# Attention with a gated mixer behind it: value projections by float32r parts, one h, one sum on ScalarE, another order at both ends

## The chip, the cores and the metric

The kernel runs on one core of a Trainium2 chip. The engines are called as in the profile: PE (TensorE, the matmuls), PEld (its weight loads), DVE (VectorE), ACT (ScalarE), POOL (GpSimd) and SP (SyncE, which issues most DMAs). The metric is the device time of one execution in microseconds, as the median of several runs.

## The reference

Four batches are computed, each with 12,288 queries of 128 channels and a field of 384 x 32 keys that is pooled 4 x 4 to 768.

```
kv_pool = mean over 4 x 4 of kv;   k = v = kv_pool @ w_sr          # 768 x 128
s = (q @ k.T) / sqrt(128);  s -= s.max(-1)
a = exp(s);  a /= a.sum(-1) + 1e-09
x = a @ v                                                         # 12288 x 128
gate = sigmoid(sum over k < 5 of conv_w[k] * x[row + k - 4])      # per channel, along the rows
out = (gate * (x @ w_val)) @ w_out
```

## The kernel before

**Tiling.** Channels lie on the 128 partitions. A group is 512 queries of one batch (24 groups per batch, 96 in all, numbered `gi`), and it has four tiles `j` of 128 queries. The loop at L655 goes through the tiles one step at a time; `mj` is the step within a group, counted one step behind `j` (`LAG`). Nothing reorders the instructions: each engine takes its own in the order in which the loop's body writes them, and the stages of one group are spread over eight passes of the loop. In the pass `gi`:

- PE makes the scores of the next tile (L358): six float32r matmuls of 384 columns, three products (high by high, high by low, low by high) for each half of the 768 keys. DVE takes the row maximum (L383), ACT the exponential with its sum (L396), DVE adds 1e-9 and scales that sum to z (L403) and inverts it (L405), ACT writes the float16 high part of the weights (L420) and DVE the low part (L424). SP transposes both by DMA (L415).
- For the group `gi - 2` PE makes av with 18 float16 matmuls of 512 columns (L436), spread over the four steps; for `gi - 3` ACT writes x (L451) into a tile that holds two groups and four columns of the group ahead (the halo).
- For the pairs of groups around `gi - 4` POOL makes the convolution: five taps (L465) and four additions (L470) of 1024 columns, over eight steps.
- For `gi - 6`, at `mj == 2`, ACT makes the tanh of the gate and PE the value projection `g_val` (L512), a float32 matmul of 512 columns; DVE makes `h = (tanh + 1) * val` (L518) in two halves of 256, at `mj` 2 and 3. For `gi - 7` PE makes the out projection (L523), ACT writes it out of PSUM (L533), and every four groups SP stores them.
- For `gi + 2` ACT and POOL split the queries: ACT casts to the high part qh (L340), POOL subtracts to the low part ql (L345).

While one batch runs, the loop slips in the set-up of the next one's keys and values piece by piece; around the change of a batch POOL has values to convert as well (L259, L262).

**Start.** Before the loop 14 pieces of keys and values are pooled and projected. `portion` turns finished pieces into keys and values: ACT writes kh (L161), DVE kl (L164), ACT the scaled values vt (L169) and their sums (L186). PE runs idle transposes in between (`warming`).

**Tail.** Behind the loop the last seven groups, n7 to n1, are written out by hand: the value and out projections that are left, av of the last two groups, the convolution of n4, n2 and n1 on ACT and DVE (L487, L491), and that of n3 on POOL (L498, L502).

Of the kernel before, what the change touches and what calls it, by code (L numbers as in the profile page):

```python
# [27 lines left out]
def attn_moe_kernel(ctx, tc, qT, kvT, w_sr, w_moe, outT):  # L28
# [37 lines left out]
    wval, wout, cwt = wm[:, 0:C], wm[:, C:2 * C], wm[:, 2 * C:]  # L66

# [200 lines left out]
    LAG = 1  # L268
# [126 lines left out]
    def expo(g, j):  # L395
        nc.scalar.activation(out=g.s[j], in_=g.s[j], func=AF.Exp, bias=g.nm.pop(j),  # L396
                             accum_out=g.z[j])

    def norm(g, j):

        g.r[j] = small.tile([P, 1], F32, name="r")
        z = small.tile([P, 1], F32, name="z")
        nc.vector.tensor_scalar(out=z, in0=g.z.pop(j), scalar1=1e-9, scalar2=2.0 ** -15,  # L403
                                op0=ALU.add, op1=ALU.mult)
        nc.vector.reciprocal(out=g.r[j], in_=z)  # L405
# [104 lines left out]

    def g_val(g, m, c0=0, c1=GQ):
        nc.tensor.matmul(m, wval, g.x[:, HALO + c0:HALO + c1], start=True, stop=True)  # L512
        return m

    def g_h(th, m, name="h", h=None):
        if h is None:
            h = work.tile([C, GQ], F32, name=name, bufs=2 if name == "h" else 1)
# [29 lines left out]
    for b in range(B):  # L547
        for i in range(NG):
            g = Group()
            g.i, g.b, g.t0, g.st = len(groups), b, i * GQ, states[b]  # L550
            g.s, g.nm, g.z, g.r, g.hl, g.pt = {}, {}, {}, {}, None, None
            g.nm2 = {}
            groups.append(g)
# [30 lines left out]
    convert = load_moe()  # L584
# [25 lines left out]
    for n, i in enumerate(order):  # L610
        pool_kv(st, i)
        finish()
        if n in (0, 6, 8):
            base, m = n, bank_pair()[:, 0] if n else misc()
        if n in ends:
            project(st, m, base * PC, ends[n] * PC, (n + 1) * PC)
        if n == 9:
            warm = misc()
        if n in (9, 10, 12):
            warming(3)  # L620
        if n == WHOLES - 3:
# [25 lines left out]
    g_ql(at(0), 2 * P, GQ)  # L647
    finish()
# [5 lines left out]
    held, CATCH_UP = [], (B - 1) * NG + 9  # L654
    for t in range(NT * G + LAG):  # L655
# [92 lines left out]
    half = GQ // 2
    two = lambda: (lambda p: (p[:, 0], p[:, 1]))(bank_pair())
    one = lambda: bank_pair()[:, 0]  # L750
# [3 lines left out]
    spare = [t[:, c:c + GQ] for t in idle for c in range(0, 3 * GQ, GQ)]  # L754

    def gate_tile(name):
        return spare.pop() if name == "th2" else work.tile([C, GQ], F32, name=name)

    def av_bank():
        return ps_av.tile([C, GQ], F32, name="av")  # L760
# [3 lines left out]
    a0, a1 = two()  # L764
    n6.m, n5.m = g_val(n6, a0), g_val(n5, a1)
    av_slice(n2, 0, 18)
    n6.th, n5.th = g_tanh(n6.gate), g_tanh(n5.gate, gate_tile("th2"))
    halo(n4, n6, nc.scalar)
    acc4 = one()
    conv_first(n4, acc4)  # L770
    n7.m = g_out(n7.h, misc())
    gate3 = conv_pool(n3)
    n6.h = g_h(n6.th, n6.m)
    n5.h = g_h(n5.th, n5.m, h=spare.pop())
    conv_rest(n4, acc4)
    new_x(n2)
    g_x(n2, n2.av)
    halo(n2, n4, nc.scalar)
    acc2 = one()
    conv_first(n2, acc2)  # L780
# [15 lines left out]
    g_x(n1, avs[0], 0, half)  # L796
    n4.m = g_val(n4, one())
    acc1 = one()
    conv_first(n1, acc1[:, :half], 0, half)
    conv_rest(n1, acc1[:, :half], 0, half)  # L800
    n2.th = g_tanh(acc2, gate_tile("th2"))
    n3.m = g_val(n3, av_bank())
    n4.h = g_h(n4.th, n4.m)
    g_x(n1, avs[1], half, GQ)
    conv_first(n1, acc1[:, half:], half, GQ)
    conv_rest(n1, acc1[:, half:], half, GQ)
    n3.th = g_tanh(gate3, gate_tile("th"))
    n2.m = g_val(n2, misc())
    n1.m = g_val(n1, one())
    n4.m = g_out(n4.h, n4.m)  # L810
    n3.h = g_h(n3.th, n3.m, h=spare.pop())
    n1.th = gate_tile("th2")
    for c in (0, half):
        g_tanh(acc1[:, c:c + half], n1.th[:, c:c + half])
    n2.h = g_h(n2.th, n2.m)
    n3.m = g_out(n3.h, n3.m)
    h = work.tile([C, 2 * GQ], F32, name="tap1", bufs=1)
    hs = [g_h(*(t[:, c:c + half] for t in (n1.th, n1.m)), h=h[:, c:c + half]) for c in (0, half)]
    out_tile(n4)
    g_evac(n4, n4.m)  # L820
    n2.m = g_out(n2.h, n2.m)
# [5 lines left out]
    for h, c in zip(hs, (0, half)):  # L827
        g_evac(n1, g_out(h, one()[:, :half]), c, c + half)
        store(n1, c, c + half)
# [28 lines left out]
```

## Time and profile before

| | |
|---|---|
| median of 3 runs | 995.91 us (995.52 to 996.45) |
| the profiled execution | 996.03 us, of which the trace's span is 994.3 |
| PE busy | 964.1 us, 97% of the span |
| DVE busy | 942.3 us, 95% |
| ACT busy | 908.7 us, 91% |
| POOL busy | 867.6 us, 87% |

A busy share is a mean over the whole span: it says neither where an engine was idle nor whether that cost time. The chain that ended last goes back from the last instruction to what released each step, so its shares tell which engine's work the end hung on. A float32 matmul of 512 columns stands in the program's order once and in the trace as two instructions ("x2").

### The profile page before, as it was taken

How to read it: one execution, taken by the hardware profiler on the slowest of the kernel's cores; microseconds unless marked ns; L12 is line 12 of the kernel's file. 1: busy time of each engine (PE TensorE's matmuls, PEld its weight loads, DVE VectorE, ACT ScalarE, POOL GpSimd, SP SyncE). 2: the span in 40 equal slices, each digit the busy share in tenths (PEclk: the TensorE clock that was granted, in tenths of full speed). 3: DMA queues.
4: the chain of work that ended last, by engine and by line, in shares of the span. 5: the costliest groups of instructions: out<-in, count | busy, mean ns of one | idle time of the engine just before them, and what ended most of it. 6: DMA issues, size and time to landing. Idle time of an engine off the chain costs nothing.

```text
span 994.3 us, 14764 instructions
## 1 busy us (share of the span) xinstructions
PE 964.1 (97%) x4523; PEld 650.2 (65%) x4523; DVE 942.3 (95%) x1934; ACT 908.7 (91%) x1599; POOL 867.6 (87%) x654
## 2 busy tenths in 40 slices
PE   4789999999999999999999999999999999999998
PEld 3566666666666666666666666666666666666664
DVE  6999999999999999999999999999999999999996
ACT  2889999999999999999999999999999999999995
POOL 2759899888999989899899998989899989988993
PEclk9899999999999999999999999999999999999999
DMA  9999999999999999999999999999999999999996
GB/s 348 270 213 226 193 174 254 237 227 228 238 252 235 242 255 223 244 227 246 219 244 240 254 240 233 240 217 223 202 218 227 201 210 250 233 203 216 190 204 169
DMA packets 610367, 227.79 MB, mean 229 GB/s; under 512 B 594544, under 2 KB 595696, under 8 KB 604528
## 3 DMA queue, kind: packets, MB, share of 16 engines
q1 hardware_dynamic: 610288, 226.84, 108.4%
q8 instruction: 37, 0.61, 0.2%
q14 instruction: 42, 0.34, 0.1%
HBM read 50.66 MB, written 25.17 MB: 76 GB/s over the span
## 4 chain that ended last, share of the span: by engine, by line
PE 87%; DVE 6%; ACT 4%; DMA 1%; issue 1%; SPq 0%; ACTq 0%; DVEq 0%
PE s L358 36%; PE av L436 35%; PE m L523 8%; PE m L512 7%; DVE hl L424 3%; ACT hl L420 2%; DMA pt<-in_kv 1%; DVE nm L383 1%; DVE pool L119 1%; ACT s L396 1%; DVE r L405 0%; DVE s L491 0%; ACT qh L340 0%; PE m L224 0%; DVE h L518 0%
## 5 line engine op out<-in xcount | busy, mean ns | idle before, releaser
L470 POOL TENSOR_TENSOR acc<-acc,tap 128x1024 f32<-128x1024 f32 x184 | 436.7, 2373 | 7.2
L436 PE MATMUL av<-pt,vh 128*128 128x512 f16 (+1 forms) x1152 | 407.9, 380 | 4.2 <-ACT x L451 4.1
L424 DVE SCALAR_TENSOR_TENSOR hl<-s,r,hl 128x768 f16<-128x768 f32 x384 | 388.2, 1011 | 9.2 <-ACT hl L420 8.7
L420 ACT ACTIVATE hl<-s,r 128x768 f16<-128x768 f32 x384 | 345.8, 900 | 45.6 <-ACT qh L340 17.7
L383 DVE TENSOR_REDUCE nm<-s 128x1 f32<-128x768 f32 x382 | 362.1, 948 | 8.9
L396 ACT ACTIVATE s<-s,nm 128x768 f32<-128x768 f32 x384 | 335.5, 874 | 8.8 <-DVE nm L393 0.9
L358 PE MATMUL s<-kh,qh 128*128 128x384 f32 x764 | 267.6, 431 | 5.5 <-DVE z L403 2.7
L436 PEld LDWEIGHTS <-vh 128*128 128x128 f16 x1164 | 113.2, 97 | 163.0 <-issue 74.0
L436 PE MATMUL av<-pt,vl 128*128 128x512 f16 (+1 forms) x576 | 217.7, 378 | 0.0
L465 POOL TENSOR_SCALAR tap<-x,wm 128x1024 f32<-128x1024 f32 x184 | 204.2, 1124 | 0.0
L358 PE MATMUL s<-kh,ql 128*128 128x384 f32 x764 | 195.3, 337 | 0.0
L358 PE MATMUL s<-kl,qh 128*128 128x384 f32 x764 | 195.3, 337 | 0.0
L358 PEld LDWEIGHTS s<-kh,qh 128*128 128x128 f32 x764 | 144.7, 191 | 62.1 <-DVE hl L424 4.8
L345 POOL TENSOR_TENSOR ql<-q,qh 128x512 fp32r<-128x512 f32 (+1 forms) x97 | 123.0, 1268 | 34.8 <-ACT qh L340 34.8
L358 PEld LDWEIGHTS s<-kl,qh 128*128 128x128 f32 x764 | 139.1, 189 | 0.0
L358 PEld LDWEIGHTS s<-kh,ql 128*128 128x128 f32 x764 | 138.7, 189 | 0.0
L436 PEld LDWEIGHTS <-vl 128*128 128x128 f16 x582 | 57.2, 98 | 86.0 <-issue 64.6
L465 POOL TENSOR_SCALAR acc<-x,wm 128x1024 f32<-128x1024 f32 x46 | 51.5, 1119 | 48.6 <-ACT x L451 48.0
L523 PE MATMUL m<-h,wm 128*128 128x512 f32 x182 | 92.9, 591 | 0.2
L512 PE MATMUL m<-x,wm 128*128 128x512 f32 x182 | 92.8, 591 | 0.0
L405 DVE RECIPROCAL r<-z 128x1 f32<-128x1 f32 x384 | 63.0, 164 | 13.2
L518 DVE SCALAR_TENSOR_TENSOR h<-th,m 128x256 f32<-128x256 f32 x180 | 74.7, 415 | 0.5 <-ACT hl L420 0.3
(110 smaller groups left out, 661.9 us busy)
## 6 DMA issues: line engine op xcount, KB each, us to landing
q<-in_q SPq DMA_DIRECT2D x23, 1024.0 KB, 5.9
out<-o SPq DMA_DIRECT2D x22, 1024.0 KB, 4.7
kvt<-in_kv SPq DMA_DIRECT2D x21, 768.0 KB, 5.3
pt<-in_kv SPq DMA_DIRECT2D x12, 384.0 KB, 7.0
o<-in_kv SPq DMA_DIRECT2D x3, 768.0 KB, 9.5
pt<-hl SPq DMA_TRANSPOSE x98, 10.1
out<-o SPq DMA_DIRECT2D x3, 512.0 KB, 2.7
kvt<-in_kv SPq DMA_DIRECT2D x2, 384.0 KB, 7.3
```

The lines of the kernel that those rows point to most:

```text
L345: nc.gpsimd.tensor_tensor(out=g.ql[:, c0:c1], in0=g.q[:, c0:c1], in1=g.qh[:, c0:c1].bitcast(F32), op=ALU.subtract)
L358: nc.tensor.matmul(g.s[j][:, h], a[:, sl], k[:, h * HALF:(h + 1) * HALF], start=(i == 0), stop=(i == 2))
L383: nc.vector.tensor_reduce(out=nm, in_=g.s[j], axis=AX.XY, op=ALU.max, negate=True)
L396: nc.scalar.activation(out=g.s[j], in_=g.s[j], func=AF.Exp, bias=g.nm.pop(j), accum_out=g.z[j])
L420: nc.scalar.activation(out=part(g, j, 0), in_=g.s[j], func=AF.Copy, scale=g.r[j])
L424: nc.vector.scalar_tensor_tensor(out=part(g, j, 1), in0=g.s.pop(j), scalar=g.r.pop(j), in1=part(g, j, 0), op0=ALU.mult, op1=ALU.subtract)
L436: nc.tensor.matmul(out, g.st[v][:, k * P:(k + 1) * P], g.pt[:, j0:j1, a * NCH + k], start=(i == 0), stop=(i == len(AV_ORDER) - 1))
L465: nc.gpsimd.tensor_scalar(out=t, in0=g.two[:, k:k + 2 * GQ], scalar1=cwt[:, k:k + 1], scalar2=1.0, op0=ALU.mult, op1=ALU.mult)
L470: nc.gpsimd.tensor_tensor(out=g.acc, in0=g.acc, in1=t, op=ALU.add)
L512: nc.tensor.matmul(m, wval, g.x[:, HALO + c0:HALO + c1], start=True, stop=True)
L518: nc.vector.scalar_tensor_tensor(out=h, in0=th, scalar=1.0, in1=m, op0=ALU.add, op1=ALU.mult)
L523: nc.tensor.matmul(m, wout, h, start=True, stop=True)
```

## The change

- **Sum on ACT.** The z of tile 1 of each group is made by ACT, right behind the exponential; that of the other three tiles stays on DVE.
- **One h.** The two halves of h become one instruction of 512 columns at `mj == 3`, and its tile has one buffer in place of two.
- **Value projections by parts.** For a chosen group (`gi` being the pass, the group is `gi - 5`) x is split into a float32r high part xh and low part xl, and the projection is three float32r products with the parts of the weights (`wvh`, `wvl`, split once on POOL). It is so for one group in four (those with `gi % 4 == 3`, 17 of them, where POOL makes xh), for every second group from group 74 on (`SUMLESS`, where DVE makes xh), and in the tail for n6, n4 and n2 (n4 and n2 with xh from ACT). POOL makes xl each time, behind ql.
- **Start.** The idle transposes of the last two pieces are issued once in place of twice, the scaling of the values of the pieces 8 to 13 goes from ACT to DVE, and the sums of that portion stand behind the last keys.
- **Tail.** The order is another: n5's value projection ahead of n6's, the out projections of n6 and n5 behind av of n1, and the store of groups 84 to 87 behind the loop.

```diff
     def expo(g, j):
         nc.scalar.activation(out=g.s[j], in_=g.s[j], func=AF.Exp, bias=g.nm.pop(j),
                              accum_out=g.z[j])
+        if j == 1:
+            z = small.tile([P, 1], F32, name="z")
+            nc.scalar.activation(out=z, in_=g.z[j], func=AF.Copy, scale=2.0 ** -15,
+                                 bias=1e-9 * 2.0 ** -15)
+            g.z[j] = z
...
+    def split_x(g, names=None):
+        if names:
+            g.xh, g.xl = (work.tile([C, GQ], F32R, name=n) for n in names)
+        else:
+            g.xh, g.xl = (work.tile([C, GQ], F32R, name=n, bufs=1) for n in ("xh", "xl"))
+        x = g.x[:, HALO:HALO + GQ]
+        if names:
+            nc.scalar.copy(out=g.xh, in_=x)
+        elif g.i < SUMLESS:
+            nc.gpsimd.tensor_copy(out=g.xh, in_=x)
+        else:
+            nc.vector.tensor_copy(out=g.xh, in_=x)
+        return lambda: nc.gpsimd.tensor_tensor(out=g.xl, in0=x, in1=g.xh.bitcast(F32),
+                                               op=ALU.subtract)
+
     def g_val(g, m, c0=0, c1=GQ):
+        if g.xh is not None:
+            for i, (w, x) in enumerate(((wvh, g.xh), (wvl, g.xh), (wvh, g.xl))):
+                nc.tensor.matmul(m, w, x, start=(i == 0), stop=(i == 2))
+            return m
...
-        warming(4)
-    finish()
+    warming(4)
+    later.pop(0)()
+    rest = later[1:]
+    later.clear()
     row_max_half(at(0), 0, 0)
+    nc.vector.tensor_scalar_mul(out=st["vt"][:, 8 * PC:WHOLES * PC], in0=late, scalar1=1.0 / RR)
     portion(3, m, WHOLES, PIECES)
...
+    later[:0] = rest
     finish()
...
-        if vg and mj > 1:
-            sl = slice((mj - 2) * GQ // 2, (mj - 1) * GQ // 2)
-            g_h(vg.th[:, sl], vg.m[:, sl], h=vg.h[:, sl])
+        if vg and mj == 3:
+            vg.h = g_h(vg.th, vg.m)
...
+        if mj == 2 and gi > 7 and (gi % 4 == 3 or gi % 2 and gi - 5 >= SUMLESS):
+            low = split_x(at(gi - 5))
...
+        if mj == 3 and low:
+            low()
+            low = None
...
-    n6.m, n5.m = g_out(n6.h, a0), g_out(n5.h, a1)
-    conv_rest(n2, acc2)
-    n4.th = g_tanh(acc4, gate_tile("th"))
-    avs = av_bank()[:, :half], misc()[:, :half]
+    n4.th = g_tanh(b[:, 0], th_tile())
     new_x(n1)
-    for n, c in enumerate((0, half)):
-        j = c // P
-        av_range(n1, avs[n], 0, len(AV_ORDER), j, j + NT // 2)
+    for m, k in ((turned, 0), (last, half)):
+        av_range(n1, m[:, :half], 0, len(AV_ORDER), k // P, k // P + NT // 2)
+    g_x(n1, turned[:, :half], 0, half)
+    conv_first(n1, a[:, 0, :half], 0, half)
+    conv_rest(n1, a[:, 0, :half], 0, half)
+    n4.m = g_val(n4, b[:, 1])
+    n2.th = g_tanh(c[:, 0], spare.pop())
+    n6.m, n5.m = g_out(n6.h, b[:, 0]), g_out(n5.h, c[:, 0])
```

PE in the loop, around the value projection of a chosen group (s are scores, m the projection's bank, av follows). Before, and after:

```order
L358 MATMUL s<-kl,qh 128x384 x2
L358 MATMUL s<-kh,ql 128x384 x2
L512 MATMUL m<-x,wm 128x512
L436 LDWEIGHTS vh
L436 MATMUL av<-pt,vh 128x512
```

```order
L366 MATMUL s<-kl,qh 128x384 x2
L366 MATMUL s<-kh,ql 128x384 x2
L544 MATMUL m<-xh,wvh 128x512
L544 MATMUL m<-xh,wvl 128x512
L544 MATMUL m<-xl,wvh 128x512
L451 LDWEIGHTS vh
L451 MATMUL av<-pt,vh 128x512
```

The one matmul became three at the same place, and its operands come from xh and xl in place of x.

POOL around the end of a pass whose group is split, where a batch begins before, in the middle of a batch after (acc and tap belong to the convolution, vh and vl to the next batch's values):

```order
L470 TENSOR_TENSOR acc<-acc,tap_2836 128x1024
L259 CAST vh<-v 128x256
L262 TENSOR_TENSOR vl<-v,vh 128x256
L345 TENSOR_TENSOR ql<-q,qh 128x512
L460 COPY x<-x 128x4
```

```order
L485 TENSOR_TENSOR acc<-acc,tap_1906 128x1024
L485 TENSOR_TENSOR acc<-acc,tap_1908 128x1024
L535 CAST xh<-x 128x512
L353 TENSOR_TENSOR ql<-q,qh 128x512
L538 TENSOR_TENSOR xl<-x,xh 128x512
L475 COPY x<-x 128x4
```

The cast stands ahead of ql and the subtraction behind it, ahead of the next pair's halo and taps.

DVE in the last stage, in the steps `mj` 2 and 3 (hl is the low part, nm the row maximum). Before, and after:

```order
L424 SCALAR_TENSOR_TENSOR hl<-s,r,hl 128x768
L403 TENSOR_SCALAR z<-s 128x1
L405 RECIPROCAL r<-z 128x1
L383 TENSOR_REDUCE nm<-s 128x1
L518 SCALAR_TENSOR_TENSOR h<-th,m 128x256
L424 SCALAR_TENSOR_TENSOR hl<-s,r,hl 128x768
L403 TENSOR_SCALAR z<-s 128x1
L405 RECIPROCAL r<-z 128x1
L383 TENSOR_REDUCE nm<-s 128x1
L518 SCALAR_TENSOR_TENSOR h<-th,m 128x256
```

```order
L439 SCALAR_TENSOR_TENSOR hl<-s,r,hl 128x768
L418 TENSOR_SCALAR z<-s 128x1
L420 RECIPROCAL r<-z 128x1
L391 TENSOR_REDUCE nm<-s 128x1
L537 CAST xh<-x 128x512
L439 SCALAR_TENSOR_TENSOR hl<-s,r,hl 128x768
L418 TENSOR_SCALAR z<-s 128x1
L420 RECIPROCAL r<-z 128x1
L391 TENSOR_REDUCE nm<-s 128x1
L552 SCALAR_TENSOR_TENSOR h<-th,m 128x512
```

The cast stands where the first half of h stood, the whole h where the second half stood.

## Rows read from the trace of the kernel before

**Rows 1.** Page: busy time by engine; chain by engine; a group with its idle.

```profile
PE 964.1 (97%) x4523; PEld 650.2 (65%) x4523; DVE 942.3 (95%) x1934; ACT 908.7 (91%) x1599; POOL 867.6 (87%) x654
PE 87%; DVE 6%; ACT 4%; DMA 1%; issue 1%; SPq 0%; ACTq 0%; DVEq 0%
...
L420 ACT ACTIVATE hl<-s,r 128x768 f16<-128x768 f32 x384 | 345.8, 900 | 45.6 <-ACT qh L340 17.7
```

**Rows 2.** Busy us by engine in two stretches; last clock, DMA share, GB/s.

```profile
core 0: us, PE busy (x) PEld busy (x) DVE busy (x) ACT busy (x) POOL busy (x), PEclk, DMA share, GB/s
85.00:245.00 160.00, 160.00 (x754) 107.99 (x753) 156.15 (x331) 150.31 (x265) 144.91 (x105) 1.00 1.08 219
755.00:965.00 210.00, 210.00 (x986) 140.93 (x985) 199.20 (x387) 200.13 (x343) 190.46 (x133) 1.00 1.06 215
```

**Rows 3.** Timeline of two groups: start, duration, engine, line, operation.

```profile
802.00 1.02 PE L512 MATMUL m<-x,wm 128*128 128x512 f32 x2
...
809.14 4.80 POOL L470 TENSOR_TENSOR acc<-acc,tap 128x1024 f32<-128x1024 f32 x2
...
811.82 1.02 PE L512 MATMUL m<-x,wm 128*128 128x512 f32 x2
...
812.95 0.42 DVE L518 SCALAR_TENSOR_TENSOR h<-th,m 128x256 f32<-128x256 f32 x1
813.29 1.01 DVE L424 SCALAR_TENSOR_TENSOR hl<-s,r,hl 128x768 f16<-128x768 f32 x1
```

**Rows 4.** Chain of waits, last stage: start, duration, engine, line, instructions.

```profile
961.73 1.31 PE av L436 x6
...
963.04 1.04 PE s L358 x6
...
967.94 0.86 PE m L512 x2
```

**Rows 5.** Groups by shape, whole run: busy time, mean ns, idle before and releaser.

```profile
L345 POOL TENSOR_TENSOR ql<-q,qh 128x512 fp32r<-128x512 f32 x95 | 121.5, 1279 | 29.3 <-ACT qh L340 29.3
...
L518 DVE SCALAR_TENSOR_TENSOR h<-th,m 128x256 f32<-128x256 f32 x180 | 74.7, 415 | 0.5 <-ACT hl L420 0.3 <-ACT th L508 0.2
...
L403 DVE TENSOR_SCALAR z<-s 128x1 f32<-128x1 f32 x384 | 57.2, 149 | 2.4 <-ACT s L396 1.2
...
L498 POOL TENSOR_SCALAR tap<-x,wm 128x512 f32<-128x512 f32 x5 | 3.4, 692 | 2.1 <-ACT x L451 1.8
...
L518 DVE SCALAR_TENSOR_TENSOR h<-th,s 128x512 f32<-128x512 f32 x2 | 1.4, 684 | 1.2 <-ACT x L458 1.2
...
L458 ACT COPY x<-x 128x4 f32<-128x4 f32 x2 | 0.4, 182 | 0.0
...
L169 ACT ACTIVATE vt<-av 128x96 f32<-128x96 f32 x1 | 0.3, 252 | 0.0
```

**Rows 6.** Timeline at the start: a DVE pair beside a POOL subtraction.

```profile
25.95 0.49 DVE L88 TENSOR_SCALAR tap<-acc 128x261 int32<-128x261 int32 x2
...
26.14 1.42 POOL L345 TENSOR_TENSOR ql<-q,qh 128x512 fp32r<-128x512 f32 x1 [2.11 <-ACT qh L340]
```

**Rows 7.** Timeline of the first keys: ACT's piece of values, and PE's first score.

```profile
21.98 0.41 ACT L169 ACTIVATE vt<-s 128x288 f32<-128x288 f32 x1 [1.25 <-DVE kl L164]
...
22.98 0.19 PEld L378 LDWEIGHTS s<-kh,qh 128*128 128x128 f32 x1 [0.69 <-ACT kh L161]
```

**Rows 8.** Chain of waits in the tail: PE's last av, DVE's next conv row.

```profile
978.96 1.98 PE av L436 x18
...
981.98 0.50 DVE s L491
```

**Rows 9.** Timeline of the tail: DVE's conv rows.

```profile
977.95 3.13 DVE L491 SCALAR_TENSOR_TENSOR s<-x,wm,s 128x512 f32<-128x512 f32 x4 [1.04 <-ACT s L487]
```

**Rows 10.** Timeline where batch two begins: POOL's ql, PE's value projection.

```profile
273.07 1.28 POOL L345 TENSOR_TENSOR ql<-q,qh 128x512 fp32r<-128x512 f32 x1
...
277.27 1.02 PE L512 MATMUL m<-x,wm 128*128 128x512 f32 x2
```

More of the change, by code (lines that the diff above doesn't have):

```diff
@@ L66, in attn_moe_kernel, with split_weights @@
     wval, wout, cwt = wm[:, 0:C], wm[:, C:2 * C], wm[:, 2 * C:]
+    wvh, wvl = (const.tile([C, C], F32R, name=n) for n in ("wvh", "wvl"))
+    def split_weights():
+        return [
+            lambda: nc.gpsimd.tensor_copy(out=wvh, in_=wval),
+            lambda: nc.gpsimd.tensor_tensor(out=wvl, in0=wval, in1=wvh.bitcast(F32),
+                                            op=ALU.subtract),
+        ]
     def load_moe():
@@ L397, in expo @@
                              accum_out=g.z[j])
+        if j == 1:
[3 more added lines that the diff above has]
+            g.z[j] = z
     def norm(g, j):
         g.r[j] = small.tile([P, 1], F32, name="r")
-        z = small.tile([P, 1], F32, name="z")
-        nc.vector.tensor_scalar(out=z, in0=g.z.pop(j), scalar1=1e-9, scalar2=2.0 ** -15,
-                                op0=ALU.add, op1=ALU.mult)
+        z = g.z.pop(j)
+        if j != 1:
+            total, z = z, small.tile([P, 1], F32, name="z")
+            nc.vector.tensor_scalar(out=z, in0=total, scalar1=1e-9, scalar2=2.0 ** -15,
+                                    op0=ALU.add, op1=ALU.mult)
         nc.vector.reciprocal(out=g.r[j], in_=z)
@@ L516, in g_h @@
         if h is None:
-            h = work.tile([C, GQ], F32, name=name, bufs=2 if name == "h" else 1)
+            h = work.tile([C, GQ], F32, name=name, bufs=1)
         nc.vector.scalar_tensor_tensor(out=h, in0=th, scalar=1.0, in1=m,
@@ L626, in attn_moe_kernel @@
             portion(cuts[n][0], m, cuts[n][1], n + 1)
+            late = m[:, :(n + 1 - cuts[n][1]) * PC]
     score_half(at(0), 1, 0)
@@ L745, in attn_moe_kernel, with th_tile @@
             store_last(held.pop(0), 4)
+    while held:
+        store_last(held.pop(0), 4)
     n1, n2, n3, n4, n5, n6, n7 = groups[:-8:-1]
     half = GQ // 2
-    two = lambda: (lambda p: (p[:, 0], p[:, 1]))(bank_pair())
-    one = lambda: bank_pair()[:, 0]
+    a, b, c = (bank_pair() for _ in range(3))
+    turned = ps_av.tile([C, GQ], F32, name="av")
+    last = misc()
     idle = [kvp.tile([C, 2, R, PC * R], F32, name="kvt").rearrange("c n r x -> c (n r x)")
             for _ in range(2)]
[L754 to L760, printed above, removed]
+    spare = [t[:, k:k + GQ] for t in idle for k in range(0, 3 * GQ, GQ)]
+    spare += [work.tile([C, 2 * GQ], F32, name="acc", bufs=2)[:, :GQ]]
+    def th_tile():
+        return work.tile([C, GQ], F32, name="th")
     new_x(n3)
     g_x(n3, n3.av)
[L764 to L767, printed above, removed]
+    n5.m, n6.m = g_val(n5, a[:, 1]), g_val(n6, a[:, 0])
+    av_range(n2, turned, 0, len(AV_ORDER))
+    n6.th, n5.th = g_tanh(n6.gate, th_tile()), g_tanh(n5.gate, spare.pop())
     halo(n4, n6, nc.scalar)
-    acc4 = one()
-    conv_first(n4, acc4)
-    n7.m = g_out(n7.h, misc())
+    conv_first(n4, b[:, 0])
     gate3 = conv_pool(n3)
-    n6.h = g_h(n6.th, n6.m)
+    n6.h = g_h(n6.th, n6.m, h=spare.pop())
     n5.h = g_h(n5.th, n5.m, h=spare.pop())
-    conv_rest(n4, acc4)
+    conv_rest(n4, b[:, 0])
+    split_x(n4, ("qh", "ql"))()
     new_x(n2)
-    g_x(n2, n2.av)
+    g_x(n2, turned)
     halo(n2, n4, nc.scalar)
-    acc2 = one()
-    conv_first(n2, acc2)
+    conv_first(n2, c[:, 0])
+    n7.m = g_out(n7.h, last)
+    conv_rest(n2, c[:, 0])
+    split_x(n2, ("qh", "ql"))()
     out_tile(n7)
@@ L783, in attn_moe_kernel @@
     store_last(n7, 2)
-    n6.m, n5.m = g_out(n6.h, a0), g_out(n5.h, a1)
-    conv_rest(n2, acc2)
-    n4.th = g_tanh(acc4, gate_tile("th"))
-    avs = av_bank()[:, :half], misc()[:, :half]
+    n4.th = g_tanh(b[:, 0], th_tile())
     new_x(n1)
-    for n, c in enumerate((0, half)):
-        j = c // P
-        av_range(n1, avs[n], 0, len(AV_ORDER), j, j + NT // 2)
+    for m, k in ((turned, 0), (last, half)):
[6 more added lines that the diff above has]
+    n6.m, n5.m = g_out(n6.h, b[:, 0]), g_out(n5.h, c[:, 0])
+    g_x(n1, last[:, :half], half, GQ)
+    conv_first(n1, a[:, 0, half:], half, GQ)
+    n3.m = g_val(n3, c[:, 1])
+    n2.m = g_val(n2, a[:, 1])
+    n1.m = g_val(n1, last)
+    n4.h = g_h(n4.th, n4.m, h=spare.pop())
+    conv_rest(n1, a[:, 0, half:], half, GQ)
     out_tile(n6)
@@ L795, in attn_moe_kernel @@
     store_last(n5, 2)
[L796 to L810, printed above, removed]
+    n3.th = g_tanh(gate3, th_tile())
+    n4.m = g_out(n4.h, b[:, 1])
     n3.h = g_h(n3.th, n3.m, h=spare.pop())
-    n1.th = gate_tile("th2")
-    for c in (0, half):
-        g_tanh(acc1[:, c:c + half], n1.th[:, c:c + half])
+    n1.th = spare.pop()
+    for k in (0, half):
+        g_tanh(a[:, 0, k:k + half], n1.th[:, k:k + half])
     n2.h = g_h(n2.th, n2.m)
-    n3.m = g_out(n3.h, n3.m)
-    h = work.tile([C, 2 * GQ], F32, name="tap1", bufs=1)
-    hs = [g_h(*(t[:, c:c + half] for t in (n1.th, n1.m)), h=h[:, c:c + half]) for c in (0, half)]
+    n3.m = g_out(n3.h, c[:, 1])
+    n1.h = work.tile([C, 2 * GQ], F32, name="tap1", bufs=1)[:, :GQ]
+    for k in (0, half):
+        g_h(n1.th[:, k:k + half], n1.m[:, k:k + half], h=n1.h[:, k:k + half])
     out_tile(n4)
     g_evac(n4, n4.m)
-    n2.m = g_out(n2.h, n2.m)
+    n2.m = g_out(n2.h, a[:, 1])
     g_evac(n3, n3.m)
@@ L826, in attn_moe_kernel @@
     store(n2)
-    for h, c in zip(hs, (0, half)):
-        g_evac(n1, g_out(h, one()[:, :half]), c, c + half)
-        store(n1, c, c + half)
+    for m, k in ((turned, 0), (b[:, 0], half)):
+        g_evac(n1, g_out(n1.h[:, k:k + half], m[:, :half]), k, k + half)
+        store(n1, k, k + half)
 def kernel(q, kv, w_sr, moe_w_val, moe_conv_w, moe_w_out):
```

11 lines of the change are left out of this document (5 added, 6 removed).

## The prediction

> **What bounds the kernel now.** I read the page first (busy shares, then the chain that ended last), then a table of busy time by stage, then the chain through the last stage. The page has four engines above 87% busy, so shares alone don't say which one counts; but the chain lies 87% of its length on PE [rows 1]. The table by stage settles it: between 85 and 245 us, and again between 755 and 965, PE is busy for the whole window, 160.00 of 160.00 and 210.00 of 210.00, at a granted clock of 1.00 (its level of 2.4 GHz), while DVE has 199.20 and ACT 200.13 of 210 [rows 2]. In the loop's steady part the time is therefore the sum of PE's matmuls. One group of 512 queries takes 9.82 us there, the distance of two value projections [rows 3]. DVE is idle for 10.8/210 × 9.82 = 0.50 us of a group, ACT for 0.46, POOL for 0.91. Ahead of about 85 us and behind about 980 us PE waits, and other engines set the end.
>
> The profiled execution took 996.03 us: a span of 994.3 and 1.73 outside it. The median of the runs is 995.91, so 0.12 comes off at the end.
>
> **Value projections in parts.** 28 of the 96 leave the single float32 matmul: 17 in the middle (one group in four), 8 at the end of the loop (every second) and 3 in the tail (the groups sixth, fourth and second from the end), so 25 in the loop. The single matmul takes 0.86 us of the chain [rows 4]. Three float32r products stand in its place. No row shows a float32r matmul of 512 columns. From one side: av's six 512-column matmuls take 1.31 us, 0.218 each; from the other, the score's six of 384 columns take 1.04, and scaled by 512/384 that is 0.231 each [rows 4]. I take 0.218, since the pace of a column falls with a matmul's width (0.173/384 against 0.218/512) and this is the row of that width. So 0.86 − 0.654 = 0.206 saved each; by the score's pace 0.167. In the loop: 25 × 0.206 = −5.15 us (−4.2 by the other).
>
> **What feeds them.** Each split adds a cast and a subtraction. The subtraction runs on POOL; its like is ql, 1.28 us [rows 5]. The cast on POOL lies by its like at 0.69 us (a scaled copy of 512). In the middle that is 1.97 us in four groups, of which POOL has 4 × 0.91 = 3.6 idle: hidden. At the end it is 1.28 us in two groups against 1.8 idle: hidden too. The values have most of a group's time to arrive, since the split of a group stands one group ahead of its projection.
> The nine casts of the last stage are on DVE. The nearest rows are its two small int32 operations, 0.49 us for both, 261 elements wide [rows 6]; by them a 512-wide copy lies between 0.25 and 0.49. DVE has 0.50 idle per group and gains the next two terms, so the copy itself is hidden. What it may wait for, I can bound only: nothing below, and above, that it waits out the add on POOL beside it. In the same group of rows a subtraction of POOL that began 0.19 us behind the DVE operation took 1.42 in place of 1.28, so one of the two does give way a little. I put 0.5 us on the end for nine copies, with 0 and 4.5 (0.5 each) as ends.
>
> **Joined h and the moved sum.** Two h of 256 at 0.415 become one of 512, 0.684 [rows 5]: DVE gains 0.146 us per group. One of four z (0.149) goes to ACT: another 0.149 for DVE. DVE isn't the bound in the loop, so both are worth 0 there; if DVE's order were late they would be its cover. The joined h ends where the second half ended, and its reader, the out projection, comes more than a group later: 0. On ACT the scaled copy of one column costs between 0.149 (DVE's own) and 0.252 (an ACT copy of 96 columns); the nearest row is ACT's 4-column copy, 0.182, and with a wait for ACT's own accumulator behind it I take 0.22. ACT's work per group goes from 200.13/210 × 9.82 = 9.36 to 9.58 us, against PE's new 9.72 to 9.77: 0 again, but with 0.14 to 0.19 us of room only.
>
> **Start.** ACT scaled a piece of the values (0.41 us) and summed it ahead of kh, and PE's first score waited 0.69 us for that kh in loading its weights [rows 7]. The scaling goes to DVE, the sums behind. ACT gets to kh up to 1.0 us sooner, but DVE takes up 0.41 us, and the stage behind it, where each tile goes round from hl to the next exp, is bound by DVE and ACT in turn. So nearly all of it may be lost: 0 to −0.6, and I take −0.25.
>
> **Tail.** The outs of the sixth and fifth group from the end (at the value projection's 0.86 each, 1.72 us) stood on PE ahead of the last av, which took 1.98 and released the last x; DVE was through with its conv rows at 977.95 + 3.13 = 981.08, but the first row for the last group could begin at 981.98 only [rows 8, 9]. With the outs behind av, and 0.206 saved on one split value ahead of it, PE would be 1.9 us earlier; DVE takes up only the 0.9 until it is busy without a gap, and from there on its rows and h's are the chain, with two more split values (0.4) beside it and not on it. The last hl still must land by DMA before av. I take −0.7, with −0.3 and −1.3 as ends.
>
> **Sum.** −5.15 + 0.5 − 0.25 − 0.7 = −5.6, so 996.03 − 5.6 = 990.4 profiled and 990.3 as the median. As a median it is 988.9 with each term at its better end (−5.15, 0, −0.6, −1.3), 995.9 with each at its worse (−4.2, +4.5, 0, −0.3). All at the worse end together is improbable; the forecast's own range is 988.6, a little beyond the better end, to 992.0.
>
> **Rivals.**
> *POOL comes late where a batch begins.* There POOL also converts values, and its rows stand close: ql ended at 273.07 + 1.28 = 274.35 and the value projection that reads x came on PE at 277.27 [rows 10]. A split puts a cast and a subtraction of 1.97 us there, so xl is ready with about 0.5 us to spare, and the taps behind are 1.97 later as well. For it: no idle time shows on POOL there; against it: the spare. If each of the three boundaries costs PE up to 1 us, the time is 992 to 993.3: still faster.
>
> *ACT becomes the bound.* Its room is 0.14 to 0.19 us per group. In favour: ACT's hl already has 45.6 us of idle time before it over the run, 45.6/96 = 0.47 per group [rows 1], so if those waits stay as they are, ACT needs 9.58 + 0.24 (half of them) = 9.82 of a group that PE ends in 9.77. Against: some of these waits are there only since ACT had time. That would return the loop to its old pace or 0.05 us above: −5.15 turns into 0 to +5, and the time into 995 to 999. The Trainium skill, "ScalarE: Activation LUTs", section "Rules for kernel authors", wants simple multiplies and adds on VectorE, not on ScalarE, and so speaks against this move: by it the time would be this rival's. The rows agree in direction (0.182 for ACT's copy, 0.149 for DVE's sum) and don't decide it.
>
> *DVE's casts wait for POOL's adds (the other side).* In the last stage the cast comes about where h stood, 812.95, while POOL's two adds run from 809.14 for 4.80 us, to 813.94 [rows 3]. If a DVE copy between two SBUF tiles can't begin until the add ends, it waits 1.0 us, and at worst a whole add of 2.4. DVE's next instructions (hl, which the transposes and then av wait for) queue behind. DVE's room in two groups is 2 × (0.50 + 0.30) = 1.6, so with the copy 1.0 + 0.45 just fits and at most 0.5 each reaches PE: 994.9. A whole add gives 2.4 + 0.45 − 1.6 = 1.25 each, 9 × 1.25 = 11 us: about 1001, slower. It decides from 0.6 us per copy on (5.6/9).
>
> The Trainium skill, "SBUF — State Buffer", section "Who interferes with whom", has this as a rule: VectorE in a two-port mode and GpSimd contend for one pair of ports, whoever issues first holds it for the whole instruction, and the other is blocked. By it the copies cost from 990.3 up to that 1001, depending on what POOL is at; the one pair of rows above (1.42 against 1.28) agrees in kind, with POOL as the one that waits.
>
> *The change doesn't do what it says:* three products need three weight loads. PEld shows 140.93 us in 985 loads, 0.143 each [rows 2], beside the matmuls. Were they no longer hidden, a split would take 3 × 0.361 = 1.08 and lose 0.22 each: 28 × 0.22 = 6.2 slower, 1002. Against it: av loads as often, for matmuls as wide, without a gap.
>
> **How the numbers follow.** Forecast 0.69; late POOL 0.12; ACT the bound 0.07; casts that wait 0.07; exposed loads 0.02; something else 0.03. This kernel's measurement can tell 0.2%, 2 us, from no change: faster is below 993.9, slower above 997.9. Faster: 0.69 + 0.12 and some of the rest, 0.83. Same: half of the ACT case, most of the casts', 0.10. Slower: 0.07. The range for 8 in 10 takes in the forecast's own and the late POOL: 988.0 to 993.8.
>
> **What would show it.** Right: three matmuls 0.22 apart for a split; PE still without a gap from 85 to about 975 and busy about 6 us less; DVE some 25 us less busy, ACT 20 more, POOL 45 more. Late POOL: PE waits before the third product, on xl, near 277 us and one and two batches (24 × 9.82 = 236 us each) later. ACT the bound: PE's scores idle, released by ACT or a chain through it. Waiting casts: the DVE cast longer than 0.5 us in the trace, or PE idle only behind 755. Wrong altogether: PE's pace per group unchanged at 9.82 with PE busy, so that a split is not cheaper than the single matmul.

## The result: 1001.89 us, slower

The changed kernel takes 1001.89 us (median of six runs, 1001.3 to 1002.53), the kernel before 996.01 on the same chips: a ratio of 1.0056, interval 1.0045 to 1.0067, so slower by some 0.6%. Forecast were 990.3 and a range of 988.0 to 993.8. The profiled execution has a span of 999.7 us against 994.3, 5.4 more.

The page of the kernel after, busy time and the chain by engine and by line (of before, without the chain by line: [rows 1]):

```profile
PE 963.3 (96%) x4547; PEld 651.5 (65%) x4547; DVE 940.2 (94%) x1758; ACT 915.5 (92%) x1696; POOL 913.0 (91%) x701
PE 86%; DVE 8%; ACT 3%; POOL 1%; DMA 1%; issue 1%; SPq 0%; POOLq 0%; ACTq 0%; DVEq 0%
PE s L366 36%; PE av L451 34%; PE m L557 8%; PE m L546 5%; DVE hl L439 3%; ACT hl L435 2%; PE m L544 2%; DVE nm L391 2%; DVE xh L537 2%; DMA pt<-in_kv 1%; POOL tap L517 1%; ACT s L404 1%; DVE h L552 0%; PE m L232 0%; PE s L557 0%
```

DVE and POOL have gained a part of the chain, and a line that is only nine instructions, DVE's xh at L537, holds 2% of it. The table by stage says where (of before: [rows 2]):

```profile
85.00:245.00 160.00, 160.00 (x761) 108.61 (x759) 153.88 (x300) 152.48 (x283) 150.88 (x111) 1.00 1.06 219
755.00:965.00 210.00, 206.32 (x962) 136.43 (x960) 199.65 (x338) 193.41 (x352) 197.51 (x140) 1.00 1.02 206
```

In the first window PE is busy throughout, as before; in the last stage it misses 3.7 us of 210, at the same clock. Where the time went can be read group by group: the out projection (L523 before, L557 after) comes once per group, so its start in the one trace less its start in the other is how far the kernel is ahead (−) or behind (+). With the groups counted from 0:

| out projection of group | 0 | 18 | 42 | 74 | 88 | end of span |
|---|---|---|---|---|---|---|
| before, us | 93.38 | 272.14 | 510.32 | 826.53 | 963.92 | 994.3 |
| after less before | +0.19 | −0.95 | −2.35 | −3.56 | +3.79 | +5.4 |

So: start +0.19, the long middle −3.75 (it does gain), the 14 groups of the last stage +7.35, the tail +1.61; together +5.40.

The groups of instructions by shape that are new or other:

```profile
L552 DVE SCALAR_TENSOR_TENSOR h<-th,m 128x512 f32<-128x512 f32 x90 | 61.0, 678 | 0.0
...
L538 POOL TENSOR_TENSOR xl<-x,xh 128x512 fp32r<-128x512 f32 x26 | 33.3, 1281 | 0.4 <-DVE xh L537 0.4
...
L537 DVE CAST xh<-x 128x512 fp32r<-128x512 f32 x9 | 16.5, 1829 | 0.0
L535 POOL CAST xh<-x 128x512 fp32r<-128x512 f32 x17 | 10.4, 611 | 0.0
```

The DVE copy of 512 columns takes 1.83 us as a mean, where the same cast on POOL takes 0.61 and the prediction had 0.25 to 0.49. The timeline of two of the nine, DVE and POOL alone (start, duration):

```profile
807.35 2.38 POOL L485 TENSOR_TENSOR acc<-acc,tap 128x1024 f32<-128x1024 f32 x1
...
809.47 0.54 DVE L537 CAST xh<-x 128x512 fp32r<-128x512 f32 x1
...
826.43 4.81 POOL L485 TENSOR_TENSOR acc<-acc,tap 128x1024 f32<-128x1024 f32 x2
...
828.95 2.58 DVE L537 CAST xh<-x 128x512 fp32r<-128x512 f32 x1
831.20 1.44 POOL L353 TENSOR_TENSOR ql<-q,qh 128x512 fp32r<-128x512 f32 x1
831.45 1.01 DVE L439 SCALAR_TENSOR_TENSOR hl<-s,r,hl 128x768 f16<-128x768 f32 x1
```

The second copy was issued just behind the start of POOL's second addition (826.43 + 2.4 = 828.83) and ended at 831.53, 0.29 behind that addition's end at 831.24. The first met the change from one addition to the next (807.35 + 2.38 = 809.73) and ended at 810.01, 0.28 behind it. In both some 0.3 us of the copy lie behind POOL's end, and the rest is the remainder of whatever POOL was at. POOL gives a little back: its ql behind the copy takes 1.44 in place of 1.28. Six of the other seven copies took 1.93 to 1.97, each begun some 0.7 us into a second addition. Behind the copy DVE's queue is late, and PE waits for it, as the waits of PE from 820 to 970 show (us in total, times, longest):

```profile
PE m L557 <- DVE h L552: 2.4, 7, 0.3
PE s L366 <- DVE z L418: 0.7, 1, 0.7
```

These are 3.1 us, less than half of what the stage lost. The matmuls overlap in the trace (av's start 0.22 us apart and are shown 0.38 long), so part of a wait lies under the end of the matmul before. The weight loads ahead of them show more of it (PEld, the same window), together 8.9 us:

```profile
PEld m L557 <- DVE h L552: 4.6, 7, 0.7
PEld s L366 <- PE av L451: 4.3, 7, 1.2
```

PE waits for h at the out projection, and ahead of a score in the same passes. The second wait is put down to PE itself, but in the pass looked at DVE's hl had ended 0.12 us before the load (853.03 and 853.15); that the score waits for hl is read from this order and not shown by itself. How little room h has, the rows of h and of its out projection show, in the kernel before and in the kernel after:

```profile
825.25 0.41 DVE L518 SCALAR_TENSOR_TENSOR h<-th,m 128x256 f32<-128x256 f32 x1
...
826.53 1.02 PE L523 MATMUL m<-h,wm 128*128 128x512 f32 x2
```

```profile
854.08 0.68 DVE L552 SCALAR_TENSOR_TENSOR h<-th,m 128x512 f32<-128x512 f32 x1
...
854.81 1.12 PE L557 MATMUL m<-h,wm 128*128 128x512 f32 x2 [0.34 <-DVE h L552]
```

Before, h ended 0.87 us ahead of its out projection (826.53 − 825.66), which is also the median of the loop; joined, it ends 0.61 ahead as a median of the kernel after, and in the passes with a late copy 0.05.

The tail, as the chain that ended last (start, duration, what):

```profile
963.12 0.69 PE m L544 x3
...
983.66 1.26 POOL tap L517
984.92 1.24 POOLq L894
...
986.21 0.50 PE s L544
986.71 1.72 PE s L557 x4
988.42 0.86 PE s L546 x2
989.28 0.71 PE s L544 x3
...
990.09 0.50 DVE s L506
```

The first row is the price of a split value in the loop, 0.69 us against 0.86 whole. In the tail POOL stands on the chain: the low part of n4 is ready only behind the convolution of n3 on POOL, PE's third product of n4 waits for it until 986.21, everything of PE's queue stands behind, and DVE's convolution rows for the second half of n1 (L506) begin at 990.09. The kernel before had them here:

```profile
984.65 2.06 DVE L491 SCALAR_TENSOR_TENSOR s<-x,wm,s 128x256 f32<-128x256 f32 x4
```

Counted from group 88's out projection, that is 22.38 us after and 20.73 before, 1.65 later: the whole loss of the tail. The rows for the first half began 0.92 earlier than before, counted in the same way (984.85 us after; 981.98 before [rows 8]): there the new order did what was forecast.

### The profile page after: what moved, and what is told of

The parts are those of the page before. It is cut to its first block, busy times and chain, and to the rows that moved or that the text cites. A ratio compares the mean times of both kernels' runs of the same rounds, so it can differ in the third digit from the quotient of the medians.

```text
span 999.7 us, 14598 instructions
## 1 busy us (share of the span) xinstructions
PE 963.3 (96%) x4547; PEld 651.5 (65%) x4547; DVE 940.2 (94%) x1758; ACT 915.5 (92%) x1696; POOL 913.0 (91%) x701
## 4 chain that ended last, share of the span: by engine, by line
PE 86%; DVE 8%; ACT 3%; POOL 1%; DMA 1%; issue 1%; SPq 0%; POOLq 0%; ACTq 0%; DVEq 0%
PE s L366 36%; PE av L451 34%; PE m L557 8%; PE m L546 5%; DVE hl L439 3%; ACT hl L435 2%; PE m L544 2%; DVE nm L391 2%; DVE xh L537 2%; DMA pt<-in_kv 1%; POOL tap L517 1%; ACT s L404 1%; DVE h L552 0%; PE m L232 0%; PE s L557 0%
## 5 line engine op out<-in xcount | busy, mean ns | idle before, releaser
L557 PE MATMUL m<-h,wm 128*128 128x512 f32 x180 | 92.5, 595 | 2.4 <-DVE h L552 2.4
L466 ACT ACTIVATE x<-av,down 128x512 f32<-128x512 f32 x96 | 65.3, 680 | 3.4 <-PE av L451 3.4
L546 PE MATMUL m<-x,wm 128*128 128x512 f32 x132 | 67.3, 591 | 0.0
```

The lines of the kernel that those rows point to most:

```text
L466: nc.scalar.activation(out=g.x[:, HALO + c0:HALO + c1], in_=av, func=AF.Copy, scale=g.st["down"])
L557: nc.tensor.matmul(m, wout, h, start=True, stop=True)
```

## The experiments

Theory L: a DVE copy between two SBUF tiles can't run beside POOL's instruction and waits for its end. Rivals: S, the rounding to float32r is slow on DVE; D, a split in every second group is too dense, whatever makes xh. All of the following are the kernel after with the edit shown; every ratio is to the kernel before on the same chip.

**e1: the nine xh by another form.**

```diff
-            nc.vector.tensor_copy(out=g.xh, in_=x)
+            nc.vector.scalar_tensor_tensor(out=g.xh, in0=at(g.i - 1).m, scalar=0.0, in1=x,
+                                           op0=ALU.mult, op1=ALU.add)
```

> The nine xh of the last stage stay on DVE, at the same place in its order, but are made by another form: 0 x (the neighbour's projection in PSUM) + x, which has one operand in SBUF in place of a copy from SBUF to SBUF. Theory L (a copy between two SBUF tiles waits until POOL's instruction ends, and DVE's queue behind it): xh takes what h of 512 columns takes, 0.68 us, in place of 1.83, DVE has room for that, and the 8.7 us that groups 75 to 88 lost (from 3.56 ahead of before to 3.79 behind, plus 9 x 0.155 not gained) go: 992.5 to 994. Rival D (density: every second group split overloads POOL or PE, whatever makes xh): 1001 to 1002.5. Rival S (the rounding to float32r is slow on DVE in any form): xh still about 1.8 us, 1001 to 1002.

Measured: 992.71 us, 0.9965 (0.9955 to 0.9975). The nine instructions, and the last stage's row of the table by stage:

```profile
L537 DVE SCALAR_TENSOR_TENSOR xh<-m,x 128x512 fp32r<-128x512 f32 x9 | 6.2, 692 | 0.0
```

```profile
755.00:965.00 210.00, 210.00 (x999) 142.29 (x998) 199.43 (x353) 201.66 (x366) 205.21 (x144) 1.00 1.05 213
```

Same engine, same place, same output type, and 0.69 us in place of 1.83, beside POOL's addition as before. PE has no gap left, at group 88 the kernel is 4.66 us ahead. S and D fall. Two things changed with this edit, the place of one operand (PSUM) and the kind of instruction, and no run takes them apart. Not every DVE instruction from SBUF to SBUF waits for POOL: the pooling of the keys in the kernel after has 120 reductions that ran beside POOL in 0.41 us each, none over 0.42.

```profile
L127 DVE TENSOR_REDUCE pool<-kvt 128x16 f32<-128x256 f32 x120 | 49.2, 410 | 0.0
```

**e2: the nine xh on POOL.**

```diff
-            nc.vector.tensor_copy(out=g.xh, in_=x)
+            nc.gpsimd.tensor_copy(out=g.xh, in_=x)
```

> The nine xh of the last stage are made by POOL, as those of the middle are. L and S: DVE loses nothing, POOL takes 0.61 more in two groups, of which it has over a microsecond idle: 993 to 994.5. D: POOL is fuller than now, 1002 or more.

Measured: 996.2 us, 1.0002 (0.9992 to 1.0011), 1.7 us above the range of L. The loop does what L says (4.55 us ahead at group 88), so density isn't it; the rest is the tail, 34.43 us from group 88's out projection to the end, where e1 has 31.64 and before 30.38: POOL comes to the tail later, and the chain of the tail goes through POOL.

**e3: the same copy, one step later.**

```diff
-        if mj == 2 and gi > 7 and (gi % 4 == 3 or gi % 2 and gi - 5 >= SUMLESS):
+        if mj == (3 if gi - 5 >= SUMLESS else 2) and gi > 7 and (
+                gi % 4 == 3 or gi % 2 and gi - 5 >= SUMLESS):
```

> The same DVE copy, one step later in the same pass, behind h, where POOL has ended its additions and waits for xh. L: it takes 0.3 to 0.5 us as POOL holds nothing, the loss goes: 993 to 995 (POOL's next taps up to 0.4 us later in a pair). S: it takes 1.8 us there too, 1000 to 1002. D: 1001 to 1002.

Measured: 995.02 us, 0.999 (0.998 to 0.9999). One of the nine, with POOL beside it:

```profile
831.55 1.28 POOL L353 TENSOR_TENSOR ql<-q,qh 128x512 fp32r<-128x512 f32 x1
...
832.48 0.64 DVE L537 CAST xh<-x 128x512 fp32r<-128x512 f32 x1
...
833.20 1.27 POOL L538 TENSOR_TENSOR xl<-x,xh 128x512 fp32r<-128x512 f32 x1 [0.36 <-DVE xh L537]
```

The very same instruction ends 0.29 us behind ql's end (832.83). It takes 0.42 to 1.06 us (median 0.51), as it meets ql's last part only; the one of 0.42, in the last of the nine passes, had POOL idle from its start to its end, and is the copy's own price. That is L and not S; at group 88 it is 4.25 ahead, and again the tail (33.33 us) takes most back, since POOL's xl waits for the copy.

**e4: the copies alone** (the values of the last stage and of n6 are whole and no xl is made for them, so nothing reads the copies).

```diff
             low = split_x(at(gi - 5))
+            if gi - 5 >= SUMLESS:
+                low, at(gi - 5).xh = None, None
```

> The last stage keeps its nine DVE copies, but no xl is made and its value projections are the single float32 matmul (the copies are read by nothing; the rest of the kernel after is kept, and n6 is whole too). L: the copies alone cost what the stage lost, 1.0 to 1.3 us each from the second on: 1001 to 1004. S: the same. D: no loss in the stage, 994 to 996.

Measured: 1000.09 us, 1.0045 (1.003 to 1.006). POOL's two additions, and the copy in the second:

```profile
846.14 4.80 POOL L485 TENSOR_TENSOR acc<-acc,tap 128x1024 f32<-128x1024 f32 x2
...
849.46 1.77 DVE L537 CAST xh<-x 128x512 fp32r<-128x512 f32 x1
```

The additions end at 850.94 and the copy at 851.23, 0.29 later. Without any split the stage loses 6.31 us (3.36 ahead at group 74, 2.95 behind at group 88), 0.94 a pair from group 76 on. The cost is the copies' alone; it is a little under the 1.0 to 1.3 that L put on each, and the kernel 0.9 us under L's range.

**e5, e6: the tail with whole values.** e5 is e1 with n4 and n2 whole; e6 has n6 whole too.

```diff
-    split_x(n4, ("qh", "ql"))()
...
-    split_x(n2, ("qh", "ql"))()
```

> e1 (xh of the last stage by the form with an operand in PSUM), and in the tail n4 and n2 are whole again, so no cast on ACT and no xl on POOL behind the convolution of n3. Theory W (in the tail PE, which takes its queue in order, stands at n4's third product until POOL, busy with n3's convolution, has made xl, and DVE's last rows wait for PE): the 1.8 and 0.8 us that DVE waits there shrink, 990.5 to 991.8 against 992.7. Rival O (the new order of the tail itself is what costs, not the split values): 992.5 to 993.5, as two whole projections are 0.3 us longer on PE.

> As e5, and n6 is whole as well, so that POOL begins the convolution of n3 some 1.3 us earlier. W: the wait was for n4's xl, which e5 took away, so no more than 0.3 us either way against e5. O: 992.5 to 993.5.

Measured: 992.77 us, 0.9961 (0.9946 to 0.9976), and 992.83, 0.9963 (0.9949 to 0.9977): no gain in time; e5 lies inside the range of rival O and outside that of W. In the traces the tail falls from 31.64 us to 31.14 and 31.28, still longer than the 30.38 of before; e5's trace also began 0.91 us later than e1's, which the edit doesn't touch. POOL is off the chain, but DVE's last rows still wait. DVE's waits from 960 us on, e6:

```profile
DVE s L506 <- PE s L547: 1.9, 1, 1.9
```

L506 are convolution rows, which need x and ACT's first tap; L547 is the value projection, which they don't read. The two share a pair of PSUM banks: the sum of n1's convolution lies in one half of `a`, n2's value projection in the other.

**e9: that projection in another bank** (on e6).

```diff
-    n2.m = g_val(n2, a[:, 1])
+    n2.m = g_val(n2, turned)
```

> e6 with n2's value projection in the bank that held av of n2 and x of n1, in place of the other half of the pair in which the convolution of n1 is summed. Theory B (in e6 DVE's last convolution rows wait 1.9 us for PE's value projections of n3 and n2 only because n2's lies in the same pair of banks, a wait that the old order did not have): the rows then wait for ACT's first tap alone, the 1.9 us go and most reach the end, 990.7 to 991.6 against 992.8. Rival (the rows are late for ACT or x anyway): 992.3 to 993.3.

Measured: 991.46 us, 0.9951 (0.9936 to 0.9966), 1.4 less than e6 by the medians; the intervals of the two overlap, so the traces have to place it. DVE's waits from 960 us on:

```profile
DVE hl L439 <- ACT hl L435: 1.0, 1, 1.0
DVE s L506 <- ACT s L502: 1.0, 1, 1.0
DVE kvt L553 <- ACT x L473: 0.9, 1, 0.9
DVE kvt L553 <- ACT th L523: 0.2, 1, 0.2
```

The rows' wait for PE is gone and the tail takes 29.96 us in place of 31.28, now 0.42 less than before. Theory B holds: with the banks apart the new order is 0.42 us better than the old, and the shared pair had cost three times that.

**e7: all sums on DVE again** (on e1).

```diff
-        if j == 1:
-            z = small.tile([P, 1], F32, name="z")
-            nc.scalar.activation(out=z, in_=g.z[j], func=AF.Copy, scale=2.0 ** -15,
-                                 bias=1e-9 * 2.0 ** -15)
-            g.z[j] = z
```

> e1 with all four sums of a group on DVE again, as before; h stays one. Theory H (PE sets the loop's pace, and neither DVE's 0.15 nor ACT's 0.17 us per group reach it): 992.4 to 993.0, PE's times in the loop the same within 0.1 us. Rival R (DVE has room for the new xh only because one sum was moved): the last stage loses again, over 0.3 us a pair, 994 or more. Rival A (ACT paid for the sum on the way): below 992.

Measured: 993.53 us, 0.997 (0.9959 to 0.9982), against e1's 992.71; the intervals overlap. The traces place a difference: between the groups 15 and 18, where the first batch changes, e1 gains 0.67 us and e7 0.33; at the second change (38 to 42) 0.65 and 0.32; at the third and everywhere else, the last stage included, they go alike. So neither H (nothing) nor R (the last stage) was right: the moved sum is worth some 0.33 us at two of three batch changes. That ACT paid for it (A) is excluded: without the sum on ACT nothing got faster.

**e12: h in two halves again** (on e1).

```diff
-        if vg and mj == 3:
-            vg.h = g_h(vg.th, vg.m)
+        if vg and mj > 1:
+            sl = slice((mj - 2) * GQ // 2, (mj - 1) * GQ // 2)
+            g_h(vg.th[:, sl], vg.m[:, sl], h=vg.h[:, sl])
```

> e1 with h in two halves again. DVE gets 0.146 us more per group. If DVE bounds nothing but the change of a batch, as e7's trace says of the moved sum (0.33 us at two of the three), 0.6 to 0.9 us more: 993.3 to 993.7, with PE's times elsewhere the same. If nothing in the loop hangs on DVE, 992.5 to 993.0. If the last stage has no room for the xh form beside two halves, 995 or more.

Measured: 995.89 us, 0.9993 (0.9984 to 1.0002): 3.2 more than e1. At the first two batch changes (groups 12 to 18, 36 to 42) it gains 0.32 and 0.31 where e1 gains 0.82 and 0.81. From group 74 to 88 it loses 0.66 where e1 gains 1.08, 0.25 us a pair, for 2 × 0.146 = 0.29 more DVE work a pair. The stage from 860 to 960, first e12, then e1:

```profile
860.00:960.00 100.00, 99.61 (x473) 67.35 (x472) 94.45 (x179) 93.91 (x173) 95.44 (x66) 1.00 1.03 203
```

```profile
860.00:960.00 100.00, 100.00 (x478) 68.29 (x477) 95.50 (x170) 95.78 (x175) 96.84 (x68) 1.00 1.01 201
```

The time is that of the case in which the last stage has no room (995 or more). In e12 PE waits while DVE shows a busy share of 94%: in this order, what DVE still shows as idle is not to be had.

**e8, e10: twelve more groups split.** e8 is e5 with these, and with every xh of the loop by e1's form on DVE, those of the middle too, which POOL made; e10 is e8 with e9's bank.

```diff
-        if mj == 2 and gi > 7 and (gi % 4 == 3 or gi % 2 and gi - 5 >= SUMLESS):
+        if mj == 2 and gi > 7 and (gi % 4 == 3 or gi % 2 and (
+                gi - 5 >= SUMLESS or gi % NG not in (NG - 3, 1))):
...
-        elif g.i < SUMLESS:
+        elif g.i < 0:
```

> e5 with twelve more groups split in the middle (every second group but the two passes around a change of batch), and every xh by the DVE form. The pace found in the trace of after is 0.155 us per split: if that is a plain price of PE, 12 x 0.155 = 1.9 us less than e5, 988.7 to 990.2. If POOL, with 168.8 of 175 us busy in the middle stage of after, can't take 1.28 us more in four groups, PE waits for x or xl there and the time is that of e5 or above.

> e8 (xh by the DVE form, twelve more groups split, n4 and n2 whole) with the same change of bank as e9: by theory B 989.0 to 990.0, by the rival 990.8 to 991.5.

Measured: 991.12 us, 0.9944 (0.9929 to 0.9959), and 990.9, 0.9946 (0.9929 to 0.9962). Both have the lowest medians of this study, with intervals that overlap e9's, and are faster than the kernels before and after; but twelve splits at 0.155 should have brought 1.9 us, and e8 lies above its range (988.7 to 990.2). From group 0 to group 88 e8 gains 5.42 and e1 4.81: 0.6 for twelve; by the medians it is 1.65 below e5, of which the traces put 0.6 down to the start. Nine of the twelve brought their 0.15 and three next to nothing, and five of the old splits fell from 0.15 to 0.03 or 0.04. In those eight groups h ended 0.18 to 0.26 us ahead of its out projection, where a median group of e8 has 0.45 and one of e1 0.61, and the out projection took 0.96 to 1.04 us in place of 0.86. So h was late there; that xh did it, with 0.69 us more on DVE, is likely and was not tested, and why in these groups and not in the others stays open. e10 expected a further 1.1 to 2.1 and has 0.2, in the rival's range; its trace has the tail of e9 (29.8 us) and lost 0.8 between the groups 77 and 78, where PE waited for a transpose.

**e11: the start as before** (on e1).

```diff
-    warming(4)
-    later.pop(0)()
-    rest = later[1:]
-    later.clear()
+        warming(4)
+    finish()
...
-    nc.vector.tensor_scalar_mul(out=st["vt"][:, 8 * PC:WHOLES * PC], in0=late, scalar1=1.0 / RR)
...
-    later[:0] = rest
```

> e1 with the start as before: ACT scales the values of the pieces 8 to 13, the sums come at once, the idle matmuls are issued twice. If the new start is worth the 0.25 us of the prediction, 992.9 to 993.2; if it costs, as the first out projection in the traces so far says (0.15 us later than before in e1, 0.3 as a mean over nine traces), 992.2 to 992.6; both ends lie near what the runs can tell, so the first out projection of the trace decides: 93.4 us before.

Measured: 993.13 us, 0.9969 (0.9957 to 0.998), against 992.71. Inconclusive: the first out projection came at 93.78 us here, and in the kernels with the new start anywhere from 92.94 (e10) to 94.44 (e5). Its trace also lost 0.55 us at group 54, where PE waited for a transpose; the edit doesn't touch that.

## Why the prediction was wrong

*The step that failed: the nine DVE copies.* The prediction had them at +0.5 us, with +4.5 as the worst end of the sum, and the copy that waits for POOL's addition as a rival with a chance of 0.07. The rival is what happened. It cost 7.35 us from group 74 to 88, and with the splits' own gain there (1.08 in e1) 8.4; e1 shows that it was all due to the form of the copy, e3 that the same copy is short where POOL is nearly through, e4 that it needs no split. The rival's price was right in kind (994.9 to 1001). That the time came out just beyond its upper end is partly chance: a copy in each of nine passes at 1.25 would have been 11 us, the copies cost 8.4, and the tail, with a smaller gain from the splits, made up the rest.

Two inputs of the rival were too kind. The wait was taken as 1.0 us, from where h stood; the copies came early in the second addition and waited 1.6 or so. And DVE's room in two groups was taken as 1.6 us, its idle time (1.0) plus what was freed (0.6). From group 76 on a pair lost 0.96 us, with the split's own gain 0.96 + 0.155 = 1.11, so of a copy of 1.94 about 0.83 was hidden; e4 gives 1.77 − 0.94 = 0.83, e12 0.69 + 0.29 − 0.25 = 0.73. That is half of the room, and since 0.59 of it was freed by the change, only 0.14 to 0.24 of the 1.0 us of idle time. It is no fixed share: e7, with 0.69 of xh and 0.30 of sums, hides 0.99 and loses nothing in that stage.

*A second step, which made the first so dear.* The prediction gave h's reader more than a group's time. But h is made in the last step of a pass, and PE makes the out projection at the start of the next, behind one tile's scores: before, it came 0.87 us behind h, and in the kernel after the joined h left 0.61. So a late DVE queue reached PE at once; PE's weight loads waited 4.6 us for h in seven passes.

The Trainium skill, "SBUF — State Buffer", section "Who interferes with whom", the rule weighed in the prediction, is what the traces show here: the copy ended 0.28 to 0.29 us behind POOL's instruction wherever it met one, and the form with one operand in SBUF (e1) ran beside POOL in 0.69. One pair of rows with 0.14 us of delay [rows 6] had been given more weight than the rule. That pair was the other order, DVE first. In the trace of the kernel after POOL's ql begins a little earlier against the same two DVE operations, and now the second of them waits, 1.36 us in place of 0.29:

```profile
25.75 1.56 DVE L96 TENSOR_SCALAR tap<-acc 128x261 int32<-128x261 int32 x2
...
25.87 1.28 POOL L353 TENSOR_TENSOR ql<-q,qh 128x512 fp32r<-128x512 f32 x1 [2.35 <-ACT qh L348]
```

*Term by term.* **Split price:** 0.155 us per split in the middle, by the steps of the out projections, in place of 0.206; three products take 0.69 to 0.71, which is the score's pace (0.231 a product) and not av's (0.218). The prediction had read the two rows as a matter of width, and the pace went with the type; its other bound, 0.167, was near. 25 × 0.155 is 3.9 in place of 5.15. **Joined h and moved sum:** costed at nothing, and worth 1.0 us where batches change (−3.75 in the middle, less 18 × 0.155 = 2.79, for 17 splits and the first of the last stage, which lies ahead of group 74's out projection): DVE held PE back there, though PE looked full (in the kernel before 59.87 of 60.00 us between 245 and 305, DVE 58.63). e7 and e12 show both as contributors, and in the last stage the joined h is the cover without which even e1 loses. ACT had the room that the prediction gave it: its sum takes 0.17 us (0.22 forecast), and in e1, with that sum on ACT, PE has no gap in the last stage. The rule on simple multiplies in "ScalarE: Activation LUTs" (the Trainium skill, section "Rules for kernel authors") would have led the wrong way here: by e7's trace the sum on ACT is 0.33 us better at two batch changes and no worse elsewhere. **Late POOL:** did not happen; in the kernel after PE is busy for 60.00 of the 60 us from 245 to 305. **Exposed loads:** no; three products took 0.69 to 0.71 and not 1.08. **Start:** +0.19 in the one trace against −0.25; between two traces it varies by more, and stays open. **Tail:** forecast −0.7, measured +1.61 (31.99 us against 30.38). Of the 2.0 us between the kernel after and e9, e1 accounts for 0.35 (the last copy stood ahead of it), e5 for 0.5 (the split values of n4 and n2), and e6 and e9 together for 1.2 (the shared pair of banks). The prediction followed what releases DVE's last rows by the data, and did not look for who else writes to the pair in which they sum. Its 0.9 us for the rows of the last group was right for the first half of them (0.92).

The forecast without the two mishaps was not far off: e9, the change with the copies' form and the bank put right and the tail's values whole, takes 991.46 us, against 990.3. Part of that is luck: the splits gave 1.3 us less than forecast, and the joined h and the moved sum 1.0 that was not in it.

## What to carry to other kernels

Before a copy between SBUF tiles is put on DVE, look at what POOL is doing at that moment, not at DVE's idle share: a form that takes one operand from PSUM (0.69 us in all nine of e1) can be cheaper than a copy that is shorter by itself (0.42 us, and 1.94 behind POOL). Idle time between dependent instructions of an engine at 95% may be of little use: here a copy found half of the room that had been counted, and a quarter of the idle time. Before such an edit, look up how far ahead of its reader each result of the engine lies; 0.87 us was all that h had, and 0.61 when joined. And when a by-hand order reassigns PSUM banks, check for each new neighbour in a tile whether its writer has now become a wait for the other half.

## What was not expected of the hardware

- The price of a DVE copy is set by the phase of POOL's instruction: 0.54, 1.94 and 2.58 us for the same copy of 512 columns, 0.28 to 0.29 behind the end of POOL's each time, and 0.42 where POOL was idle (e3).
- Which of two operations waits can differ from trace to trace: of the twelve kernels with the new start the second DVE operation of the pair in [rows 6] waited in five (1.36 us in place of 0.29, ql 1.28), and in the other seven ql gave way (1.41 to 1.43).
- A float32r product of 512 columns takes 0.23 us of PE's chain, a float16 one of the same width 0.218.
- The start, in kernels that share its code, came out up to 1.5 us apart from trace to trace (first out projection 92.94 to 94.44 us), more than the 0.25 us forecast for the edits made there.
